# Neighbouring operands for the matmuls, with small masks, a product for b and a new issue order, in a kernel of windowed attention and a gated MLP

## The chip, the cores and the metric

The kernel runs on one core of one Trainium2 chip. The metric is the device time of one execution in microseconds (us); smaller is better. Every ratio below is made with runs of the kernel before on the same chip in the same session. Each run carries a state: slow means that it was over 1.5% above the fastest run of the same kernel. Differences in us between two changed kernels are of medians, mostly from different sessions.

## The reference, cut to what matters

```python
# 8 batches, 8 heads, 576 positions, 64 per head
mask_plain = (rel >= 0) & (rel < 32)                      # heads 0..3, "plain"
mask_dil   = (rel >= 0) & (rel < 128) & (rel % 4 == 0)    # heads 4..7, "dilated"
attn = softmax(where(mask, q @ k.T / 8, -1e9));  x = attn @ v        # -> (8, 576, 512)
h = gelu_tanh(x @ w_in);  u, v = halves of h
v_n = layer_norm(v) * g_ln
v_s = w_sg @ v_n + b_sg                                   # over positions, 576 x 576
out = x + (u * v_s) @ w_out
```

Positions are kept in "residue order" (all with rest 0 by 4, then rest 1, ...), because the dilated heads see every fourth position.

## The kernel before

Each step is a small function, and a string, the plan, lists the steps in the order in which they are issued. Each engine is given its own share of them in that order. These names are needed below:

- `iLVP:b`, `iLVH:b`: load v of the plain heads of batch b, and its 32 halo rows, through SyncE's queue, in pieces of 256 bytes (a row of 64 fp32), 2304 and 736 of them. `VC:b`: ScalarE casts both to fp16. There is one staging buffer, so batch 1's load waits for batch 0's cast.
- `iLQ..`, `iLK..`, `iLW..`: the larger loads through GpSimd's queue. `iMSK` masks, `iBG` b and g.
- `R` transposes of q and k, `S` scores, `E` exp, `M` mask product, `AS` sums, `AV` products with v, `NX` division (its result is xT), `zv`, `zu` products with w_in, `sgr`, `sgu` products with w_sg, `out` products with w_out and the residual, `O` copy of the result out of PSUM, `iD` store. `w:n` are n products of zeros that keep the clock up. `@n` names a PSUM slot.

```python
def VC(b):
    nc.scalar.copy(vps[b % 2]..., vst)                     # one vst for all batches
def E(b, g, hf, x):                                        # scores -> probabilities
    nc.scalar.activation(PT[:, :, HS*hf:HS*hf+HS], pss[:, :, 0:HS], AF.Exp, scale=0.125)
def AV(b, g, x):   # plain heads: every fourth probability is read
    nc.tensor.matmul(o[...], v_half, PT[:, QB*s:QB*s+QB].rearrange("p (m u) -> p u m", u=4))
def out_(b, ti):
    for ph in range(4): nc.tensor.matmul(po[...], gat[:, ph, ts], w_out16[:, ph, :])
    for g4 in range(4):                                    # residual: every second column of po
        nc.tensor.matmul(po[...].rearrange("p (w x) -> p x w", x=2)[:, g4 % 2, :], xT[:, g4, ts], ident16)
osbs = ring("osb", 3, ...)                                 # three output buffers
```

The softmax here doesn't subtract the row's maximum and nothing guards it: scores larger than these inputs give would overflow.

## Time and profile before

| | before |
|---|---|
| median, two runs | 230.32 us (229.77 to 230.87) |
| span of the profiled run | 229.2 us |
| TensorE, VectorE, ScalarE, GpSimd busy | 92%, 75%, 64%, 30% |
| first product with w_in (`pz`), by the timeline | 27.1 us |

The page's busy shares and its chain are shown in the prediction. Two lines of the page's groups are added here, since the change rewrites what they read. The columns are line, engine, operation, output and input, their shapes and count, then busy us and mean ns, then idle time just ahead of them. The exp of the scores and the copy of the result both read PSUM in order:

```profile
L292 ACT ACTIVATE PT<-pss 128x576 f16<-128x576 f32 x64 | 38.0, 651 | 24.7 <-PE pss L288 24.6
L487 ACT COPY osb<-po 128x1024 f32<-128x1024 f32 x16 | 16.2, 1016 | 19.9 <-PE po L468 18.7
```

And this table of stretches (first column the stretch, then its length, then busy us and count for TensorE, its weight loads, VectorE, ScalarE and GpSimd, then the clock, the DMA share and GB/s) shows that the transfers run at some 200 GB/s from 20 to 35 us while TensorE has work nearly all the time:

```profile
20.00:25.00 5.00, 4.94 (x71) 2.04 (x70) 1.59 (x3) 4.57 (x8) 2.65 (x5) 0.78 1.14 213
25.00:30.00 5.00, 3.97 (x82) 1.99 (x74) 4.13 (x7) 2.48 (x4) 0.00 (x0) 1.00 1.12 203
30.00:35.00 5.00, 5.00 (x25) 2.25 (x23) 3.37 (x10) 3.36 (x4) 3.42 (x5) 1.00 1.10 201
```

### The profile page before, as it was taken

What the parts mean: (1) busy time and instruction counts of PE and PEld (TensorE: products, weight loads), DVE (VectorE), ACT (ScalarE), POOL (GpSimd) and SP (SyncE); (2) the same over time, 40 slices, a digit from 0 to 9 for tenths busy, and PEclk for the clock granted to TensorE, in tenths of its full rate; (3) what the DMA queues carried; (4) which work ended last, traced back from release to release, by engine and by line L of the source; (5) the groups of instructions that cost most, each with busy time, mean ns of one, the idle gap of its engine ahead of it and who ended that gap; (6) DMA issues with size and microseconds to landing.
All of it is one profiled execution on the core that took longest, in us unless ns stands there. A gap on an engine that the chain in (4) does not pass through costs nothing.

```text
span 229.2 us, 6969 instructions
## 1 busy us (share of the span) xinstructions
PE 209.8 (92%) x3020; PEld 131.5 (57%) x3020; DVE 171.2 (75%) x314; ACT 147.3 (64%) x201; POOL 67.8 (30%) x131
## 2 busy tenths in 40 slices
PE   7627896998999999999999999999999999999990
PEld 2223444765657566565565676666656655766650
DVE  2487478898768999899879989988955668686400
ACT  2068658678685598778979973756788785721231
POOL 8244057602017061922029364050000003420000
PEclk9955999799999999999999999999999999999998
DMA  8999997993917979998849999026076430000354
GB/s 157 205 216 212 208 205 136 171 158 57 219 22 102 209 220 171 142 190 124 246 69 223 215 216 195 8 44 212 3 125 159 159 114 3 0 1 3 114 169 128
DMA packets 45326, 31.68 MB, mean 138 GB/s; under 512 B 30048, under 2 KB 36704, under 8 KB 45296
## 3 DMA queue, kind: packets, MB, share of 16 engines
q0 software_dynamic: 13984, 14.95, 41.6%
q1 hardware_dynamic: 31312, 16.29, 29.4%
q8 instruction: 23, 0.38, 0.7%
q14 instruction: 7, 0.06, 0.1%
HBM read 36.75 MB, written 9.44 MB: 202 GB/s over the span
## 4 chain that ended last, share of the span: by engine, by line
PE 71%; DMA 9%; DVE 9%; ACT 4%; POOL 2%; issue 2%; ACTq 1%; DVEq 0%; POOLq 0%
PE po L465 13%; PE pg L443 11%; PE pz L367 11%; PE pu L421 10%; PE po L468 6%; DMA qkp<-in_k_dram 5%; PE pss L288 4%; DMA qkd<-in_k_dram 4%; PE pav L310 4%; PE psu L338 3%; DVE vs L449 2%; PE po L475 2%; PE pg L436 2%; PE pav L321 2%; PE pb L507 2%
## 5 line engine op out<-in xcount | busy, mean ns | idle before, releaser
L292 ACT ACTIVATE PT<-pss 128x576 f16<-128x576 f32 x64 | 38.0, 651 | 24.7 <-PE pss L288 24.6
L421 PE MATMUL pu<-xT,w_in 128*128 128x288 f16 x256 | 35.4, 292 | 0.0
L443 PE MATMUL pg<-wsgT,vn 128*128 128x288 f16 x256 | 35.4, 287 | 0.0
L465 PE MATMUL po<-w_out,gat 128*128 128x512 f16 x128 | 33.5, 384 | 0.0
L449 DVE SCALAR_TENSOR_TENSOR vs<-pg,g_col,b_bc 128x576 f16<-128x576 f32 x32 | 25.5, 804 | 9.3 <-PE pg L443 9.2
L367 PE MATMUL pz<-w_in,xT 128*128 128x512 f16 x128 | 29.7, 380 | 0.0
L421 PEld LDWEIGHTS <-w_in 128*128 128x128 f16 x256 | 25.0, 100 | 7.9 <-issue 0.3
L487 ACT COPY osb<-po 128x1024 f32<-128x1024 f32 x16 | 16.2, 1016 | 19.9 <-PE po L468 18.7
L443 PEld LDWEIGHTS <-vn 128*128 128x128 f16 x256 | 23.2, 98 | 9.6 <-issue 3.8
L426 ACT ACTIVATE u<-pu 128x576 f16<-128x576 f32 x32 | 19.9, 650 | 12.7 <-PE pu L421 12.5
L406 POOL TENSOR_SCALAR rs<-mv 128x2 f32<-128x2 f32 (+1 forms) x24 | 7.0, 292 | 67.2 <-DVE mv L393 62.4
L297 DVE TENSOR_TENSOR PT<-PT,masks 128x1152 f16<-128x1152 f16 x32 | 22.8, 748 | 1.4 <-ACT PT L292 1.3
L388 DVE BATCH_NORM_STATS2 st<-vv 128x6 f32<-128x512 f32 x32 | 21.5, 671 | 3.2 <-ACT vv L378 3.1
L378 ACT ACTIVATE vv<-pz 128x1024 f32<-128x1024 f32 x16 | 16.3, 1025 | 9.3 <-PE pz L367 7.2
L412 DVE TENSOR_SCALAR vn<-vv,mv,rs 128x512 f16<-128x512 f32 (+1 forms) x40 | 19.2, 507 | 3.2 <-POOL rs L407 3.2
L367 PEld LDWEIGHTS <-xT 128*128 128x128 f16 x128 | 12.0, 99 | 13.3 <-issue 0.6
L468 PE MATMUL po<-ident,xT 128*128 128x128 f16 x128 | 19.2, 304 | 0.0
L352 DVE TENSOR_TENSOR xT<-pav,rsum 128x576 f16<-128x576 f32 x16 | 11.6, 752 | 8.6 <-PE pav L310 5.0
L407 POOL TENSOR_TENSOR rs<-rs,mhalf 128x2 f32<-128x2 f32 (+1 forms) x24 | 17.4, 723 | 2.0
L507 PE MATMUL pb<-zeros 128*128 128x512 f16 x60 | 16.8, 433 | 1.2 <-DVE zeros L170 1.2
L465 PEld LDWEIGHTS <-gat 128*128 128x128 f16 x128 | 12.3, 107 | 9.2 <-issue 0.4
L468 PEld LDWEIGHTS <-xT 128*128 128x128 f16 x128 | 13.2, 118 | 7.6
(68 smaller groups left out, 311.5 us busy)
## 6 DMA issues: line engine op xcount, KB each, us to landing
vst<-in_v_dram SPq DMA_DIRECT2D x8, 576.0 KB, 9.0
qkp<-in_q_dram POOLq DMA_DIRECT2D x8, 288.0 KB, 5.9
qkp<-in_k_dram POOLq DMA_DIRECT2D x8, 288.0 KB, 8.0
qkd<-in_q_dram POOLq DMA_DIRECT2D x8, 288.0 KB, 6.3
qkd<-in_k_dram POOLq DMA_DIRECT2D x8, 288.0 KB, 7.5
vm<-in_v_dram POOLq DMA_DIRECT2D x8, 256.0 KB, 6.7
out_dram<-osb SPq DMA_DIRECT2D x8, 256.0 KB, 3.5
out_dram<-osb SPq DMA_DIRECT2D x8, 224.0 KB
```

Source lines behind the costliest of these rows:

```text
L292: nc.scalar.activation(PTb[4 * (b % 2) + 2 * g + x][:, :, HS * hf:HS * hf + HS], live["pss", b, g, hf][x][:, :, 0:HS], AF.Exp, scale=0.125)
L297: nc.vector.tensor_tensor(PT, PT, masks[:, p // 2, :].unsqueeze(1).broadcast_to([KB, 2, S]), AO.mult)
L367: nc.tensor.matmul(pz[:, ti % 2, :], xT[:, g4, 128 * ti:128 * ti + 128], w_in16[:, g4, DH:DFF], start=(g4 == 0), stop=(g4 == 3))
L388: nc.vector.bn_stats(s, vvs[(3 * b + i) % 4][:, c, :])
L412: nc.vector.tensor_scalar(vns[b % 2][:, ti, 0:n], vvs[(3 * b + i) % 4][:, c, 0:n], live["mv", b, i][:, c, 0:1], live["rs", b, i][:, c, :], ...
L421: nc.tensor.matmul(pu[:, j, 0:HS], w_in16[:, g4, 128 * ph:128 * ph + 128], xT[:, g4, HS * j:HS * j + HS], start=(g4 == 0), stop=(g4 == 3))
L426: nc.scalar.activation(us[b % 2][:, ph, :].rearrange("p (j w) -> p j w", j=2), live.pop(("pu", b, ph))[:, :, 0:HS], AF.Gelu_apprx_tanh)
L443: nc.tensor.matmul(pv[:, j, 0:HS], vns[b % 2][:, kp, 128 * ph:128 * ph + 128], wsgT16[:, kp, HS * j:HS * j + HS], start=False, stop=(kp == 3))
L449: nc.vector.scalar_tensor_tensor(vs.rearrange("p (j w) -> p j w", j=2), live.pop(("pg", b, ph))[:, :, 0:HS], g_col[:, ph:ph + 1], b_bc.rea ...
L465: nc.tensor.matmul(po[:, ti % 2, :], gat[:, ph, ts], w_out16[:, ph, :], start=(ph == 0), stop=False)
L468: nc.tensor.matmul(po[:, ti % 2, 256 * (g4 // 2):256 * (g4 // 2) + 256].rearrange("p (w x) -> p x w", x=2)[:, g4 % 2, :], xT[:, g4, ts], i ...
L507: nc.tensor.matmul(pb[:, 0, :], zeros[:, 0:128], zeros, start=True, stop=True)
```

## The change

The intent is to let the matmuls read and write neighbours. The strides are moved to engines that were thought not to mind: the exp of the plain heads reads PSUM at a stride and writes residue order; w_out's columns are permuted once by GpSimd, so that the residual falls on neighbouring columns, and the copy out puts the columns back. Masks are loaded small (88 KB, not 288) and spread by VectorE; b comes as one row and is spread over the partitions by two products. With it comes a wholly new plan, in which batches 0 and 1 both go through attention before batch 0's big products.

```diff
 def E(...):
+    if g == 0:                                  # plain heads: write residue order
+        dst = dst.rearrange("p h (u m) -> p h u m", u=4); src = src.rearrange("p h (m u) -> p h u m", u=4)
 def AV(...):                                    # AS likewise
-    PT[:, QB*s:QB*s+QB].rearrange("p (m u) -> p u m", u=4)
+    PT[:, HS*(s//3):...].rearrange("p (u m) -> p u m", u=4)[:, :, 24*(s%3):24*(s%3)+24]   # runs of 24
 def out_(...):
-    po[...].rearrange("p (w x) -> p x w", x=2)[:, g4 % 2, :]
+    po[:, ti % 2, 128*g4:128*g4+128]
+def WO():   # GpSimd, once: w_out16[.. (x c)] = loaded[.. (c x)], two copies
+def MX():   # VectorE, once: five copies build the mask table from a small row
+def PB():   # TensorE, once: ones1 (1 x 128) times b_row (1 x 576), two fp32 products
 def O(...):
-    nc.scalar.copy(osb, po)
+    nc.scalar.copy(osb.rearrange("p c (g w x) -> p (c g) w x", ...), po.rearrange("p c (g x w) -> p (c g) w x", ...))
 PLAN
-ew iLQP:1 iLKP:1 iLQD:0 ... iMSK iLVP:0 iLVH:0 ... VC:0 ... zv:0:4@1 ... zu:0:3 ... iLVH:1 iLVP:1 ... VC:1 ... AV:1:0:1@1 ... zv:1:0
+ew iLVP:0 iLKD:0 iBG ... iLVH:0 VC:0 ... iMSK MX iLVH:1 iLVP:1 ... VC:1 ... AV:1:0:1@1 AV:1:0:0@0 ... W:0:4@0 zv:0:0@1 ...
... (the rest of the plan is new as well)
```

## The prediction

> **What bounds the kernel now.** I read the page first (busy shares, the slices, the chain of waits), then the chain in order of time, then stretches of the timeline on TensorE, because the diff rewrites access patterns that only matmuls and ScalarE see. The page:
>
> ```profile
> PE 209.8 (92%) x3020; PEld 131.5 (57%) x3020; DVE 171.2 (75%) x314; ACT 147.3 (64%) x201; POOL 67.8 (30%) x131
> ...
> DVE  2487478898768999899879989988955668686400
> ...
> PEclk9955999799999999999999999999999999999998
> ...
> PE 71%; DMA 9%; DVE 9%; ACT 4%; POOL 2%; issue 2%; ACTq 1%; DVEq 0%; POOLq 0%
> ```
>
> TensorE carries 71% of the chain that ends last, and the DMA share of it is the start. VectorE is the next engine: its row shows eights and nines through the middle, so it has little slack there. The clock row shows the TensorE clock at half speed at the beginning, where the array has too little work.
>
> The question is then what a matmul costs, and a busy time with the pipeline's latency in it does not say. The chain does, since it counts a matmul only until the next one takes over:
>
> ```profile
> 113.87 0.97 PE po L465 x4
> 114.84 0.44 PE po L468 x4
> ```
>
> Four output products of 512 columns take 0.86 to 0.97 us, about 0.216 us each; four residual products (L468, xT times the identity) of only 128 columns take 0.44, so 0.109 each. By columns they should take 0.055. They write every second fp32 of PSUM. Two more pairs from the timeline (start, length to the modelled end):
>
> ```profile
> 182.66 0.69 PE L338 MATMUL psu<-PT,ones 128*32 128x288 f16 x8
> ...
> 184.24 0.45 PE L338 MATMUL psu<-PT,ones 128*32 128x288 f16 x8
> ```
>
> The same eight sums of 288 columns take 0.69 us where they read every fourth fp16 (the plain heads) and 0.45 where they read neighbours (the dilated heads).
>
> ```profile
> 181.24 0.71 PE L310 MATMUL pav<-PT,vp 128*32 128x96 f16 x24
> ```
> ```profile
> 88.63 0.44 PE L288 MATMUL pss<-qTp,kTp 32*128 32x96 f16 x24
> ```
>
> Both are 24 matmuls of 96 columns in sets of four that run side by side. The products with v, which read every fourth probability, take 0.71 us; the score products, whose operands are contiguous, 0.44.
>
> Are the residual products held up by their weights instead, one load for each? The transposes of w_sg answer: each has its own 128-column weights too, and eight of 72 columns run in one piece.
>
> ```profile
> 37.27 0.43 PE pw L251 x8
> ```
>
> With some 0.17 us of that being the last one's drain, about 0.033 us each: a weight load can be hidden in 0.033 us, so it does not explain 0.109. The stride does.
>
> **What the Trainium skill says.** (1) "PSUM — Partial Sum Buffer", Specifications: PSUM has 8-byte lines, and a pattern that is not contiguous slows matmuls markedly. The residual writes (8-byte stride, 0.109 against 0.055 us) agree. (2) "SBUF — State Buffer", the paragraph on cachelines under Door 1: 16-byte lines, two hits on a line needed for full rate. The trace agrees that a stride hurts but puts the edge lower: an 8-byte stride has two hits on a line and still halves the rate (0.69 against 0.45). (3) "TensorE: Matmul & The Clock Gate", the section on 56 ns: warm, N columns take N/2.4 ns plus 2.5. That gives 216 ns for 512 columns, which the chain shows, and 56 for 128. (4) "ScalarE: Activation LUTs", on the exp ACTIVATE: 0.833 ns an element whatever the function. The trace: (1016 - 651) ns / (1024 - 576) = 0.815. No page says what a strided PSUM read costs ScalarE.
>
> **The change part by part.**
>
> *Residual products.* w_out's columns are permuted once, so the residual goes to 128 neighbouring columns. 128 matmuls save 109 - 56 = 53 ns: 6.8 us. The last 64 rows of a batch have 32 more, running two at a time: 16 pairs at about 53 ns, 0.8 us.
>
> *Sums of the plain heads.* 8 batches, each 0.69 - 0.45 = 0.24 us: 1.9 us.
>
> *Products with v, plain heads.* 384 matmuls = 16 groups of 24, each 0.71 - 0.44 = 0.27 us: 4.3 us. (Runs of 24 neighbours are left, 48 bytes; I count those as contiguous.)
>
> Sum on TensorE: 6.8 + 0.8 + 1.9 + 4.3 = 13.8 us of array time, spread over every batch.
>
> *Warm-up products.* 60 become 35. They stand mostly in gaps; those after 29 us (13 + 2 + 6) delay work, at 0.216 us each 4.5 us, and the new plan has only two or four there.
>
> *Exp.* The 32 exps of the plain heads now read PSUM at a stride of four fp32; the 24 copies of the result read it at 512 bytes. Same element counts. The strided matmul writes move 128 elements in 0.107 to 0.109 us, so PSUM serves about 1.2 scattered fp32 a ns, and ScalarE wants 1.2. I expect 651 and 1016 ns to stay, with up to 10% as an estimate.
>
> *Masks.* The load falls from 288 KB to 88. Five VectorE copies build the whole table: 1152 elements, as one mask product (748 ns) plus four more starts: 1.2 us once. The 32 mask products stay.
>
> *b.* A broadcast load of 288 KB becomes one row and two fp32 products at the start, perhaps 1 to 2 us in a place where TensorE only warms up.
>
> *w_out.* Two GpSimd copies of 1024 elements per partition, at the 2273 ns / 2304 of its w_sg copy about 1 us each; GpSimd is at 30% and the copy comes well before the first output product. Nothing on the path.
>
> *The plan.* Every engine's order is new. Both batches 0 and 1 now go through attention before the first big product. Before, the first pz stands at 28.7 us. After, it waits for w_in's second half, behind eight q/k loads, vm, wsg and vt. The fp32-to-fp16 loads land about 1.6 us apart (q at 8.2, k at 9.8, then 11.4, 13.0, 14.7, 16.2 in the trace), so eight end near 16.5 + 1.6 = 18 us and the rest of that queue (about 1.4 MB as written at 0.19 MB/us, from the GB/s row) near 26 to 30. So the big products start near 30 us, not earlier, but with 1 to 2 us more attention done, and the stretch from 31 to 52, where before had about 5 us of gaps, 3 of warm-up and half clock, gets denser: only the half-clock loss (about 2) and some 2 to 3 of gaps should remain there. I put the start's gain at 5 us (2 to 8).
>
> *Does 13.8 arrive?* By 31 us the new plan has VectorE through eight loads' transposes (8 x 1.35), the mask copies (1.2), b (0.9), eight mask products (6.0), six xT products (4.5) and the memsets (1.6): 25 us. That leaves 147 of 172, in some 168 us up to its last product if the end is near 208: 88%. Before, from 45 us on, it had 142 left in 171: 83%. It is not the bound, but short waits for pg, pav and vs evacuations will grow. I take 75 to 80% of the 13.8, near 11 us, and something for the fuller ScalarE.
>
> Time: 230.3 - 11 - 5 = 214; without any loss 230.3 - 13.8 - 7 = 209.5. I choose 212.
>
> **The rivals.** *A, ScalarE slows on strided PSUM reads.* If the stride halves its rate as it does TensorE's: 32 x 0.47 + 16 x 0.85 = 29 us more, 176 of about 212. ScalarE would be near-bound, and every exp latency longer. For: the PSUM lines. Against: its rate is just the scattered rate seen. Time then 218 to 226.
>
> *B, VectorE becomes the bound.* For: its row of nines. Then the gain in the middle is only a third to a half of 13.8, and the end 218 to 221.
>
> *C, the mask load blocks the start.* VectorE has the mask copies ahead of the plain heads' transposes, and the small load stands in the same queue behind v in 256-byte pieces. In before, ident (32 KB) took 13.5 us there:
>
> ```profile
> ident<-ident SPq DMA_DIRECT2D x1, 32.0 KB, 13.5
> ```
>
> For: that line. Against: v is now asked for first, before the other queue is running, and b's and the old mask's bytes are gone; I expect the mask near 13 us and 2 us of idle VectorE. If it comes at 18, the scores of batch 0 slip by 4 to 5 us, but the products wait for w_in anyway, so the end moves by 1 to 3.
>
> *D, the weights bind the residual after all*: 0.1 us each, and 6 of the 13.8 us vanish: near 218. The w_sg products speak against it.
>
> **Range and chances.** The stride gain is measured within this kernel, so a gain over 2% (below 225.7) needs most rivals to fail together before it is lost. Range 204 to 221. Faster 0.95, same 0.04, slower 0.01.
>
> **What would show it.** Four residual products in about 0.22 us of chain and 0.39 of timeline (with drain); 24 v products in about 0.44; all eight-sum groups at 0.45; exp mean at 650 to 720 ns and copy mean near 1016; first pz near 30 us; VectorE share above 80%; TensorE still first in the chain. I am wrong if the residual keeps 0.1 us (D), the plain exps show 1.1 us (A), or VectorE leads the chain after 60 us (B). An end below 204 would mean that the new plan closed gaps that I left in.

## More of the kernel before

The chain of waits in order of time (start, length, what) shows how early the big products begin, and when ScalarE casts batch 1's v (the first `pz`, at 27.1 us, is a small one):

```profile
29.04 3.57 PE pz L367 x16
...
53.78 1.37 ACT vp L197
```

Batch 1's v is cast at 53.8 us, more than 20 us after batch 0's big products began.

## The result, and the profile after

| | before | after |
|---|---|---|
| median, two runs | 230.32 us | 241.28 us (241.22 to 241.35) |
| span of the profiled run | 229.2 us | 239.4 us |
| mean granted clock | 0.965 | 0.91 |
| TensorE busy | 209.8 us | 197.4 us |
| first product into `pz` | 27.1 us | 51.2 us |
| from there to the end | 202.1 us | 188.2 us |

The change made the kernel slower: ratio 1.048, interval 1.037 to 1.058. A ratio here is the mean time of one kernel's fast runs over that of the kernel before in the same rounds, so it is not quite the ratio of the medians. The last two rows split the result: the part after the first big product is 13.9 us shorter, and that product comes 24.1 us later. The difference, 10.2 us, is that of the spans.

The page of the kernel after, in the lines that answer to those of before:

```profile
PE 197.4 (82%) x2999; PEld 123.9 (52%) x2999; DVE 172.9 (72%) x320; ACT 146.5 (61%) x201; POOL 69.6 (29%) x133
...
PEclk9975555557999999999999999999999999999998
...
PE 56%; DMA 19%; DVE 9%; ACT 9%; issue 3%; SPq 1%; ACTq 1%
...
L317 ACT ACTIVATE PT<-pss 128x576 f16<-128x576 f32 x64 | 38.0, 651 | 14.0 <-PE pss L309 13.7
...
L509 ACT COPY osb<-po 128x1024 f32<-128x1024 f32 x16 | 16.3, 1016 | 13.6 <-PE po L493 8.4
```

The strided PSUM reads cost ScalarE nothing that can be seen here: 651 and 1016 ns are the means of before to the nanosecond. TensorE's share of the chain falls from 71% to 56%, DMA's rises from 9% to 19%, and the half clock lasts six slices in place of two.

TensorE's side came out as meant. Four residual products take 0.22 us of the chain where they took 0.44, and each lasts 219 ns where it lasted 314. In the timeline (start, length to the modelled end) the 24 products with v now take 0.43 to 0.44 us, where they took 0.71, and the eight sums 0.41 to 0.43, where they took 0.69:

```profile
83.54 0.97 PE po L490 x4
84.51 0.22 PE po L493 x4
```
```profile
175.11 0.41 PE L363 MATMUL psu<-PT,ones 128*32 128x288 f16 x8
175.36 0.43 PE L334 MATMUL pav<-PT,vp 128*32 128x96 f16 x24
```

The loss is at the start. The chain of waits in order of time:

```profile
3.81 13.26 DMA vst<-in_v_dram
17.17 1.48 ACT vp L197
...
19.05 24.06 DMA vst<-in_v_dram
43.19 1.48 ACT vp L197
44.71 1.15 PE pav L334 x48
...
51.30 3.53 PE pz L392 x8
```

Read it from the top. The halo rows of batch 0's v are asked for at 3.8 us and land at 17.2. ScalarE casts them; this is its first work in the new order. Only then is the staging buffer free, so batch 1's v is asked for at 19.05 and lands at 43.2. ScalarE stands before that cast, TensorE before the products that need it, and the first big product starts at 51.3. The waits of the first 60 us (total, times, longest) name the same three things:

```profile
ACT vp L197 <- DMA vst<-in_v_dram: 22.1, 2, 15.2
...
PE pav L334 <- ACT vp L197: 9.1, 1, 9.1
DVE masks L233 <- DMA mrow<-band_masks: 9.1, 1, 9.1
```

The small masks stand behind v's halo in the same queue; VectorE stood idle for 9.1 us until they came at 19.0. What the engines did meanwhile:

```profile
35.00:40.00 5.00, 0.58 (x8) 0.05 (x8) 2.10 (x3) 1.19 (x2) 1.27 (x2) 0.50 1.15 207
40.00:45.00 5.00, 0.29 (x16) 0.29 (x20) 0.00 (x0) 1.81 (x2) 0.00 (x0) 0.50 1.11 206
45.00:50.00 5.00, 4.53 (x118) 3.06 (x109) 2.67 (x4) 4.92 (x6) 0.00 (x0) 0.50 1.20 193
```

TensorE is busy for 0.58 and 0.29 of 5 us, but the DMA engines are not idle; they move 200 GB/s as before. v gets a poor part of it. In the first 45 us of the trace GpSimd's queue (q0) and SyncE's (q1) moved (packets, MB, share of the engines' time):

```profile
q0 software_dynamic: 5450, 7.03, 88.6%
q1 hardware_dynamic: 6466, 1.68, 23.3%
```

Counted by the microsecond in the trace's DMA records, SyncE's pieces of 256 bytes went at 830 to 990 a microsecond while they were alone (at 2 to 4 us), and at 85 to 92 from 8 to 15 us, when GpSimd's queue put 76 to 82 pieces of 2304 bytes through in the same time. The Trainium skill, "DMA: Bandwidth & Descriptors", section "Queues, rings and completion order", says that a DMA engine serves its queues in turn, packet by packet. The equal counts fit that, if a turn carries as many pieces on one queue as on the other (no run here shows what a turn carries): the queue of small pieces then moves a ninth of the bytes. Batch 1's v fared little better. Asked for at 18.7 to 19.1 us, its 3040 pieces went at 77 to 388 a microsecond from 22 to 37 us, when the other queue's pieces were mostly smaller too, and the last 140 or so took from 37 to 43 us.

A second loss is in the middle, where the outputs of two batches come close together. ScalarE waits for an output buffer that the store has not freed:

```profile
126.13 9.14 DMA out_dram<-osb
...
135.37 1.02 ACT osb L509
136.43 3.61 PE pz L392 x16
```

### The profile page after: what moved, and what is told of

It reads as the page before. It is cut to its first block, busy times and chain, and to the rows that moved or that the text cites.

```text
span 239.4 us, 6940 instructions
## 1 busy us (share of the span) xinstructions
PE 197.4 (82%) x2999; PEld 123.9 (52%) x2999; DVE 172.9 (72%) x320; ACT 146.5 (61%) x201; POOL 69.6 (29%) x133
## 3 DMA queue, kind: packets, MB, share of 16 engines
q0 software_dynamic: 13984, 14.95, 39.1%
## 4 chain that ended last, share of the span: by engine, by line
PE 56%; DMA 19%; DVE 9%; ACT 9%; issue 3%; SPq 1%; ACTq 1%
DMA vst<-in_v_dram 16%; PE pg L468 12%; PE pz L392 11%; PE pu L446 9%; PE po L490 8%; DMA out_dram<-osb 4%; PE pss L309 3%; PE pg L461 2%; PE po L493 2%; ACT vp L197 2%; ACT osb L509 2%; ACT L537 2%; PE pz L396 2%; ACT PT L317 2%; PE pav L334 1%
## 5 line engine op out<-in xcount | busy, mean ns | idle before, releaser
L392 PE MATMUL pz<-w_in,xT 128*128 128x512 f16 x128 | 32.4, 401 | 3.3 <-ACT osb L509 3.3
L490 PE MATMUL po<-w_out,gat 128*128 128x512 f16 x128 | 33.0, 380 | 1.7 <-ACT osb L512 1.2
L446 PE MATMUL pu<-xT,w_in 128*128 128x288 f16 x256 | 33.5, 286 | 0.0
L321 DVE TENSOR_TENSOR PT<-PT,masks 128x1152 f16<-128x1152 f16 x32 | 25.6, 821 | 8.3 <-ACT PT L317 8.1
L451 ACT ACTIVATE u<-pu 128x576 f16<-128x576 f32 x32 | 19.8, 653 | 12.2 <-PE pu L446 9.9
L197 ACT CAST vp<-vst 128x1536 f16<-128x1536 f32 x8 | 11.8, 1473 | 22.1 <-DMA vst<-in_v_dram 22.1
L509 ACT COPY osb<-po 128x1024 f32<-128x1024 f32 x16 | 16.3, 1016 | 13.6 <-PE po L493 8.4
L392 PEld LDWEIGHTS <-xT 128*128 128x128 f16 x128 | 12.3, 102 | 17.4 <-issue 5.9
L437 DVE TENSOR_SCALAR vn<-vv,mv,rs 128x512 f16<-128x512 f32 (+1 forms) x40 | 18.7, 493 | 1.1 <-POOL rs L432 1.1
L309 PE MATMUL pss<-qTd,kTd 32*128 32x128 f16 (+1 forms) x512 | 9.1, 200 | 9.2 <-ACT PT L317 7.9
L490 PEld LDWEIGHTS <-gat 128*128 128x128 f16 x128 | 10.9, 98 | 11.0 <-issue 1.7
L334 PE MATMUL pav<-PT,vp 128*32 128x96 f16 x384 | 7.5, 225 | 9.1 <-ACT vp L197 9.1
## 6 DMA issues: line engine op xcount, KB each, us to landing
qkd<-in_k_dram POOLq DMA_DIRECT2D x8, 288.0 KB, 10.2
```

The costliest lines, as they stand in the source:

```text
L321: nc.vector.tensor_tensor(PT, PT, masks[:, p // 2, :].unsqueeze(1).broadcast_to([KB, 2, S]), AO.mult)
L392: nc.tensor.matmul(pz[:, ti % 2, :], xT[:, g4, 128 * ti:128 * ti + 128], w_in16[:, g4, DH:DFF], start=(g4 == 0), stop=(g4 == 3))
L437: nc.vector.tensor_scalar(vns[b % 2][:, ti, 0:n], vvs[(3 * b + i) % 4][:, c, 0:n], live["mv", b, i][:, c, 0:1], live["rs", b, i][:, c, :], ...
L446: nc.tensor.matmul(pu[:, j, 0:HS], w_in16[:, g4, 128 * ph:128 * ph + 128], xT[:, g4, HS * j:HS * j + HS], start=(g4 == 0), stop=(g4 == 3))
L451: nc.scalar.activation(us[b % 2][:, ph, :].rearrange("p (j w) -> p j w", j=2), live.pop(("pu", b, ph))[:, :, 0:HS], AF.Gelu_apprx_tanh)
L490: nc.tensor.matmul(po[:, ti % 2, :], gat[:, ph, ts], w_out16[:, ph, :], start=(ph == 0), stop=False)
```

## The experiments

All kernels gave correct results but two that leave batch 1's v out. "Before" stood at 230.8 to 231.5 us in these sessions. The table has the times; the text below has the edits and what follows. First `pz` is of the profiled run. Of the six runs each of p3 and e11 one was slow; the fast ones alone have medians of 222.88 and 223.28.

| run | median us | ratio to before, interval | first pz, us |
|---|---|---|---|
| after | 241.28 | 1.048 (1.037 to 1.058) | 51.2 |
| e1 patterns, masks and b, old order | 224.36 | 0.973 (0.966 to 0.980) | 28.3 |
| e2 old patterns, new order | 247.95, one fast run | none | 53.2 (slow) |
| e3 halo load first | 234.0 and 234.5 fast | 1.015 (1.006 to 1.024) | 50.9 (slow) |
| e4 clock kept up | 242.10 | 1.049 (1.042 to 1.056) | 51.7 |
| e5 first wait moved | 244.72 | 1.060 (1.054 to 1.066) | 55.3 |
| e6 second wait moved | 236.15 | 1.022 (1.016 to 1.028) | 43.9 |
| e7 both moved | 230.4 and 231.9 fast | 1.001 (0.994 to 1.008) | 39.1 (slow) |
| e8 six output buffers | 235.67 | 1.018 (1.011 to 1.025) | 51.1 |
| e9 batch 1's v not loaded | 234.05 | 1.013 (1.008 to 1.018) | 43.4 |
| e10 both moved further, six buffers | 232.05 | 1.004 (1.002 to 1.006) | 35.2 |
| p1 residual alone, old order | 224.97 | 0.973 (0.969 to 0.978) | 27.0 |
| p2 exp's order alone, old order | 225.5 and 226.9 fast | 0.979 (0.973 to 0.985) | 26.0 |
| p3 both patterns, old order | 223.24 | 0.962 (0.957 to 0.967) | 27.0 |
| e11 as e1, six output buffers | 223.63 | 0.968 (0.963 to 0.973) | 27.7 |
| e12 none of the waits | 221.09 | 0.957 (0.953 to 0.961) | 36.1 |
| e13 batch 1 later | 231.77 | 1.003 (0.999 to 1.008) | 35.6 |

### Order or patterns: e1 and e2

The theory was that the order loses and the patterns gain. The rival was that the patterns themselves hurt. e1 puts every new pattern, the masks and b into the old plan; e2 is the kernel before with the new plan.

```diff
 e1 = after, with before's PLAN:  +iMSK MX (first)   -w:5@2 +PB@2 BG   +WO (ahead of out:0:0)
 e2 = before, with after's PLAN:  -PB@0 -MX -WO
```

> All of the changed code (contiguous residual, exp in residue order, small masks, b by a product, w_out permuted once), issued in the order of the kernel before. Theory A (the new access patterns pay as counted, and the new order of the first 57 us loses it): 217 to 223 us, 4 to 5% faster than before. Rival B (the new patterns cost something that takes their gain back, e.g. on ScalarE or VectorE): 229 us or more.

> The old code in the new order (steps of the new code that do not exist in it are left out). Theory A: slower than the changed kernel by about what the patterns are worth, 250 to 256 us. Rival B: about 240 us, as the changed kernel.

e1 is 6.4 us faster than before. The direction is as expected; the size is less than half of the 13.8 us of array time, and 224.4 lies just outside the expected 217 to 223. e2 is far slower than before. Three of its four runs were slow, so its 247.95 rests on one, but that is 17 us above before with the same patterns. Both agree: the order loses, the patterns gain. From e1 to after only the plan differs, and that costs 16.9 us by the medians (224.36 to 241.28).

### What in the order: e3 and e4

e3 asks for the halo rows right behind v, ahead of the b row. e4 fills the gaps with products of zeros, to see whether the half clock is the cause rather than a sign.

```diff
 e3:  -iLVP:0 iLKD:0 iBG ... iLVH:0      +iLVP:0 iLVH:0 iLKD:0 iBG
 e4:  -w:3@3 +w:33@3    +w:40@1 (ahead of AV:1:0:1@1)
```

> The changed kernel with one load moved: v's halo rows of batch 0 are asked for directly behind v's main rows, before b, g, ident and the masks. Theory A (the halo's 736 pieces of 256 bytes get into the queue after the other queue has started, land at 17.2 us, hold ScalarE's first instruction, and so push batch 1's v to 43 us): the first v cast starts near 8 us instead of 17.2, the second ends near 30 instead of 44.7, TensorE's 9.3 us wait before batch 1's products is gone, total 222 to 230 us. Rival C (the new order is poor throughout, the start is only a part of it): 236 to 241 us.

> The changed kernel with 70 more warm-up products in TensorE's two long waits, and nothing else. Rival D (the half clock from 15 to 56 us, for want of warm-up products, is the loss by itself): 233 to 237 us. Theory A (the waits are the loss, the clock only adds to it): 238 to 241 us.

e3 missed in its mechanism: the halo still landed at 17.0 us (16.96 for its cast), since v's main rows fill their queue until the fifth microsecond and the other queue's pieces start in the same one; batch 1's v landed at 43.2. It also made a new wait: TensorE stood 9.0 us for the b row, which now came behind the halo. Its two fast runs are nevertheless 7 us below after; the profiled run is a slow one (240.07), so why is not shown. In e4 the mean clock rose from 0.91 to 0.941, with two slices at half clock in place of six and the full clock from 40 us on, and the time stayed at 242. So the half clock goes with the idle array and is not the cause by itself.

### The two waits: e5, e6 and e7

e5 loads the masks first and puts the first cast behind the first exps. e6 lets batch 0's first big products go ahead of the second cast and of what needs it. e7 does both.

```diff
 e5:  +iMSK (first)   -iLVH:0 VC:0 +iLVH:0   -iLVH:1 iLVP:1   E:0:1:1:1 +VC:0 iLVH:1 iLVP:1
 e6:  -VC:1 -AV:1:0:1@1 AV:1:0:0@0 -NX:1:0:1 -NX:1:0:0
      zv:0:1 ... Gz:0:0 +VC:1 iLVH:2 iLVP:2 ... +AV:1:0:1@3 NX:1:0:1 AV:1:0:0@0 NX:1:0:0 AV:1:1:1@3
 e7 = e5 and e6
```

> The changed kernel; the masks are asked for first of all, and the first v cast (with the loads behind it) stands behind the first five exps on ScalarE instead of ahead of them. After the miss of the halo experiment I think that batch 1's v (3040 pieces of 256 bytes, asked for after the first cast, landing near 43 us) is what binds. Theory A2: the scores of batch 0 run 5 to 7 us earlier, but the wait for the second cast stays and grows, and the total stays at 238 to 242 us. Rival (the first wait is on the path): 232 to 236 us.

> The changed kernel; batch 1's v cast and the products that need it stand behind batch 0's first pz products instead of ahead of batch 0's sums, w_sg transposes and pz. The loads are as they were. Theory A2: TensorE's 9 us wait at 35 us goes, the first pz comes at 40 to 42 us instead of 51, total 230 to 235 us. Rival C (poor order throughout): 238 us or more.

> Both moves together. Theory A2: each removes what the other leaves, the first pz comes at 31 to 35 us and the total is 222 to 229 us. If it is no better than the second move alone, the first wait never mattered.

e5 alone read 3.4 us more, though its interval overlaps that of after; its first big product came 4.1 us later. With the first cast later, batch 1's v was asked for later, and TensorE stood 17.9 us for the second cast. The first wait was hidden behind the second. e6 alone gave 5.1 us (236.15, just above the expected 230 to 235), both together about 10 by two fast runs of four, with the first big product at 39. e7's 231 is outside the expected 222 to 229. So the waits are real and stand one behind the other, and a repair of one shows only what the next leaves over.

### Buffers: e8

```diff
-osbs = ring("osb", 3, ...)     osbs[(3*b + i) % 3]
+osbs = ring("osb", 6, ...)     osbs[(3*b + i) % 6]
```

> The changed kernel with six buffers for the output instead of three. In it, ScalarE waits 5.1 us for output transfers at 126 to 136 us and TensorE 1.5 and 3.4 us behind it. Theory E (a second loss of the new order: the outputs of batches 1 and 2 are bunched and their buffers come free late): those waits go and the total falls by 4 to 6 us, to 235 to 237. Rival: the later work is limited elsewhere, under 2 us gained.

It gave 5.6 us, and the stretch from 120 to 140 us shows where. First after, then e8:

```profile
120.00:140.00 20.00, 15.37 (x263) 9.01 (x262) 14.44 (x27) 14.35 (x20) 6.06 (x11) 1.00 0.85 179
```
```profile
120.00:140.00 20.00, 19.83 (x353) 12.39 (x353) 18.84 (x38) 18.68 (x27) 7.25 (x16) 1.00 0.97 214
```

TensorE was busy for 15.4 of 20 us and is now for 19.8. The output buffers were a cause of their own.

### The second wait taken away, and a first attempt at a repair: e9 and e10

e9 does not load batch 1's v at all (a wrong result, relative error 0.31), so the second cast waits for nothing. e10 puts the first cast just ahead of the products that need it, with the masks first, e6's move and six buffers.

```diff
 e9:   -iLVH:1 iLVP:1
 e10:  +iMSK (first)  -VC:0 ... iLVH:1 iLVP:1  +VC:0 iLVH:1 iLVP:1 (ahead of AV:0:0:0@0)  + e6 + e8
```

> The changed kernel without the two loads of batch 1's v (its cast reads batch 0's v again, so the result is wrong on purpose); nothing is moved. Theory A2: ScalarE's second wait for v and TensorE's 9 us wait behind it vanish, the first pz starts near 42 us instead of 51, total 230 to 234 us. If the order of the steps were to blame and not the data coming late, it stays above 238.

> The changed kernel with both v casts moved behind what does not need them (the first one further back than in the run with both moves) and six output buffers. Theory A2 with E: the gains add, 8 us and 5.6 us: 225 to 230 us, at best equal to the changed patterns in the old order (224).

e9 gained 7.2 us, and in its chain in order of time the first wait now leads, as the load of the masks behind v and its halo:

```profile
0.73 5.71 DMA vst<-in_v_dram
...
6.46 12.46 DMA mrow<-band_masks
```

So with batch 1's v out of the way the first big product still comes at 43.4 us. e10 was a miss: 232.05, no better than before, although its first big product comes at 35.2 us. Its chain says why:

```profile
22.20 26.66 DMA vst<-in_v_dram
48.94 1.48 ACT vp L196
50.46 0.70 PE pav L333 x19
```

The load asked for 3 us later lands 6 us later, at 48.9, and the wait has moved to just behind the first big products.

### What was still open: e12 and e13, p1, p2, p3 and e11

Two questions remained: are these waits the whole loss, and why did e1 gain only 6.4 us of 13.8?

e12 takes the three waits away at once (no load of batch 1's v, masks first, late first cast, six buffers; a wrong result). e13 is a correct kernel that moves batch 1's cast and products with v down to just ahead of batch 1's own big products.

```diff
 e12:  +iMSK (first)  -VC:0 -iLVH:1 iLVP:1  +VC:0 (ahead of AV:0:0:0@0)  + e8
 e13 = e10, and VC:1 AV:1:0:1 AV:1:0:0 AV:1:1:1 AV:1:1:0 with their NX moved to ahead of zv:1:0@0
```

> The changed kernel with the mask load first, v's first cast behind the exps, six output buffers, and batch 1's v not loaded at all (wrong result on purpose). It bounds what the named waits cost together. If they are the whole loss of the new order, it reads 214 to 220, near what was predicted. If the new order costs something by itself, 223 to 229.

> The same with v loaded, and batch 1's cast and products with v moved behind batch 0's big products, to just before batch 1's own. v then has until about 60 us. If the late v of batch 1 is what kept the earlier repair at 232, it reads 219 to 226 and the first big product starts before 34 us. If not, 230 or more.

e12 reads 221.1 us, 20.2 below after, and that is more than the 16.9 that the order lost (e1 to after). So taking the named waits away removes the whole loss of the new order. It does not reach the 214 to 220 that was expected for this case, nor fall in the 223 to 229 of its rival: 221.1 lies between. A lighter load of the queues is not what helped: in the first 45 us they moved 6.82 and 1.68 MB, against 7.03 and 1.68 in after, since batch 2's v now followed at 27.9 us. But e12 is a wrong kernel, and no correct one here is rid of the waits. In its chain no transfer holds the start, and the first big products stand at 36 us:

```profile
34.45 1.73 PE pw L271 x26
36.18 3.53 PE pz L391 x8
```

e13 missed. The plan lets batch 1's big products alternate with batch 0's, so "just ahead of batch 1's" is still only 5 us later than batch 0's first ones. v landed at 48.5 and TensorE stood again (same columns as above, second figure TensorE):

```profile
35.00:40.00 5.00, 5.00 (x37) 2.23 (x36) 2.94 (x5) 0.87 (x1) 0.94 (x2) 0.61 1.14 208
40.00:45.00 5.00, 1.75 (x14) 0.67 (x12) 2.10 (x6) 0.54 (x2) 1.31 (x4) 1.00 1.10 201
45.00:50.00 5.00, 0.00 (x0) 0.00 (x0) 0.00 (x0) 1.45 (x2) 0.00 (x0) 0.57 0.57 95
```

Three placements of the request, at 19.05, 22.20 and 22.06 us, gave landings at 43.2, 48.9 and 48.5. TensorE stands for it from 35.6 us in after, 39.7 in e10 and 41.8 in e13, and has it in none of them by then. The order of before asks for it at 23.1 us, later still, but casts it at 53.8.

For the second question, p1 is the kernel before with the residual's neighbours (and w_out's permutation) alone, p2 with the exp's order alone, p3 with both, all with the old plan, masks and b. e11 is e1 with six output buffers.

```diff
 p1 = before + out_, O, WO of after      p2 = before + E, AV, AS of after (constant mask table in residue order)
 p3 = p1 + p2                            e11 = e1 + e8
```

> The kernel before with only the contiguous residual (w_out permuted once, put back by the copy out), old order. By the array time: 7.6 us at most, by the share that arrived of the whole in the old order (6 to 7.5 of 13.8) 3.5 to 4: 225 to 228 us.

> The kernel before with only the residue order made by the exp (masks permuted in the constant, sums and v products reading neighbours), old order. By the array time: 6.2 us at most, by the share that arrived about 3: 226 to 229 us.

> The kernel before with its own order, masks and b; both the contiguous residual and the residue-order exp are in, so it is the full set of patterns without the small masks and without b by a product. If the two patterns simply do not add in this order (the time freed is lost to other waits), it reads 224 to 225, as with masks and b. If masks or b's product at half clock cost something at the start, it reads 219 to 222.

> The changed patterns in the old order (224.4 in an earlier call) with six output buffers in place of three. If output buffers take back part of the gain, as the 3.6 us wait for out_dram in that trace suggests, it reads 219 to 222. If the rest of the lost gain is elsewhere, 223.5 to 225.

With 231.3 us for before, the ratios mean 6.2 us for p1 and 4.8 for p2 (two of its four runs were slow). By the prediction's sum p1 frees 6.8 + 0.8 = 7.6 us of the array and p2 1.9 + 4.3 = 6.2, so 81% and 77% arrive, with wide intervals (5.2 to 7.1 us and 3.4 to 6.2). p3 gains 8.8 us of 13.8 (7.5 to 10.1), or 64%. The two halves make 11.0 us when added; given the intervals, whether they add is not settled. p3 and e11 ran in one session, at 0.962 and 0.968 with overlapping intervals. p3's 223.24 lies between its two expected ranges. Whether the small masks and b's products cost a microsecond in the old order is therefore not settled, and neither is whether the six buffers helped e11 over e1. The page of p3 shows what took the rest, its chain by engine:

```profile
PE 48%; DVE 18%; DMA 11%; ACT 10%; POOL 6%; issue 3%; SPq 1%; ACTq 1%; POOLq 0%; DVEq 0%
```

TensorE leads the chain for 48% of the span where it led for 71%, VectorE for 18% where it had 9%, and ScalarE for 10% where it had 4%. A faster array waits more often for its operands. That is read from the shares and was not tried by an experiment.

## Why the prediction was wrong, point by point

**The array's time: right.** The residual products, the sums and the products with v all fell to the predicted lengths (0.22, 0.41 to 0.43 and 0.43 to 0.44 us). (The 56 ns for 128 columns was an estimate from the page's rule; four in 0.22 us are 55 each.) The best check is p3, whose order and warm-up products are those of before: its page's groups fall from 19.2 to 12.4 us (residual), 3.1 to 2.3 (its last rows), 8.9 to 7.1 (sums) and 10.4 to 6.0 (products with v), 13.8 us in all. (In after TensorE's busy time fell by 12.4 us, but 6.0 of that are fewer warm-up products, and the half clock made other products longer.) The weight loads stayed, 128 before and after, so the strides were the cause and rival D falls.

**ScalarE on strided PSUM reads: right.** 651 and 1016 ns, unchanged. Rival A falls. The reason given, that PSUM serves scattered elements just as fast as ScalarE wants them, was not tested.

**"75 to 80% arrives, near 11 us": off in size.** For each half alone it held (81% and 77%). For both together, in the old order, 8.8 of 13.8 us arrived, 64%. Rival B, VectorE as the bound, does not fall with this: in p3 VectorE leads the chain for 18%, though TensorE still leads it for 48%. And in the new order VectorE is busy for 39.6 of the 40 us from 60 to 100 (after; 39.5 in e12), where it had 34.2 before and 35.6 in p3. What it costs there was not tried.

**Masks, b, w_out: right in cost, wrong in place.** The five mask copies take 0.17 to 0.28 us each, b's products 1.2 us (2.3 in e1) and GpSimd's two w_out copies 2.0 us together (in e1). But the load of the small masks came at 19.0 us, not 13. Rival C foresaw a load at 18 and priced it at "1 to 3" us, because "the products wait for w_in anyway". They did not. w_in's second half was asked for at 13.6 and 15.2 us, with a longest landing of 14.7 us for such loads, so it was there by 30 us. The scores, their masks and v were late instead. What this first wait is worth was not isolated. Of the 20.2 us that e12 wins, e9 has 7.2 and e8 5.6, which leaves 7.4 for it by subtraction, or 6.1 by the ratios of the sessions; it is a rough figure, and supposes that the three add.

**"I put the start's gain at 5 us": this step failed.** It was reasoned that "the big products start near 30 us, not earlier", from the loads on GpSimd's queue alone. (The 28.7 us that it gives for before is the chain's first `pz`; the timeline has one at 27.1.) The path through SyncE's queue was not followed: v's halo, the first cast, the freed staging buffer, batch 1's v, the second cast, the products with v. In the new order this path is 43 us long before the second cast, and that cast stands ahead of the big products in the queues of both ScalarE and TensorE. The first of these came at 51.2 us. Nor was the second consequence of the order seen, two batches' outputs close together on three buffers, which cost 5.6 us (e8). In place of a gain of 5 us the order gave a loss of 16.9 us (e1 to after, where only the plan differs).

**Would the order have gained without its waits?** Little. With the same code and six buffers, e12 is 2.6 us below e11 by the ratios (0.957 and 0.968, intervals apart), half of the predicted 5, and e12 is spared a wait that a correct kernel would have to hide. Against p3 it is level: the spans of e12 and p3 are 219.3 and 219.2 us. e12 needs 183.2 us from its first big product to its end against p3's 192.2, but starts it at 36.1 against 27.0. The 9 us that the new order wins later are lost at the start.

**What stays open.** Why e3's fast runs are 7 us below after is not explained, since its profiled run was slow. The share of the first wait is a subtraction. Neither a second staging buffer for v nor v in larger pieces, the two repairs that this path suggests, was tried. The part of the patterns' gain that does not arrive was placed by the chain's shares alone.

The best correct kernel is p3, 223.24 us, 3.8% below before by the ratio and 7.5% below after by the medians: both patterns, the old order, the old masks and b.

## What to carry to other kernels

When a change bundles new access patterns with a new issue order, count the patterns by the array's time, but follow every load of the new order from its request to the first engine that has to wait for it, on every queue, small ones too. Here a load in small pieces beside a queue of large ones got few bytes, so what mattered was less when it was asked for than how late the order could afford to need it. Repair waits together or take them away in one kernel that may be wrong: a single repair shows only what the next wait leaves over.

## What the Trainium skill lacked or had wrong

- "SBUF — State Buffer", on cachelines under Door 1: two hits on a 16-byte line are said to be enough. A matmul operand of fp16 at a stride of 8 bytes has two hits and still ran at about half rate: eight sums took 0.69 us so and 0.41 to 0.45 with neighbours.
- "PSUM — Partial Sum Buffer" and "ScalarE: Activation LUTs": neither says what a strided PSUM read costs ScalarE. Here nothing to be seen: 651 ns either way for the mean exp (half of them read at a stride of four fp32 in the kernel after), 1016 ns either way for the copy, read at a stride of 512 bytes in the kernel after.
- "DMA: Bandwidth & Descriptors", section "Queues, rings and completion order": it says that queues take turns by packet, but gives no figure for a queue of small pieces beside one of large ones. Here 256-byte pieces fell from 830 to 990 a microsecond alone to 85 to 92 beside 76 to 82 pieces of 2304 bytes.
- "SBUF — State Buffer", section "Who interferes with whom": right, with a number to add. It says that a VectorE instruction with two SBUF inputs contends with a GpSimd one that reads SBUF. In after one mask product took 3.12 us in place of 0.75 while GpSimd made a copy of 2.26 us; 0.75 + 2.26 is 3.01. In e5 and e12, with the same copy, the longest took 2.45 and 2.58.
